# Where the sums of the second weights are made: three quarters moved between VectorE, GpSimd and their places in the order

## The chip, the cores and the metric

The kernel runs on one core of a Trainium2 chip. The metric is the device time of one execution in microseconds (us). The kernel before takes 844.11 us, the median of three runs (843.39, 844.11, 844.64). Five engines work side by side: PE (TensorE, the matmuls), DVE (VectorE), ACT (ScalarE), POOL (GpSimd) and SP (SyncE, which here issues nearly all DMA transfers, one after the other in program order).

## What is computed

Attention inside chunks of 64 positions, then a residual feed-forward layer behind a normalisation, all in float32:

```python
# q, k, v: 8 batches x 8 heads x 576 positions x 64
scores = scale * np.matmul(q_c, k_c.transpose(0, 1, 2, 4, 3))   # 9 chunks of 64
attn = np.exp(scores - np.max(scores, axis=-1, keepdims=True))
attn = attn / (np.sum(attn, axis=-1, keepdims=True) + 1e-09)
x = heads side by side of np.matmul(attn, v_c)                  # 8 x 576 x 512
mu = np.mean(x, axis=-1, keepdims=True)
var = np.mean((x - mu) ** 2, axis=-1, keepdims=True)
xn = (x - mu) / np.sqrt(var + 1e-06) * g_ln
ch = np.maximum(xn @ w_ch1, 0.0) @ w_ch2                        # 512 -> 2048 -> 512
return x + ch
```

(The line on x is put in words.)

## The kernel before

**Tiles.** The 4608 rows are 18 pairs of 256 rows, two pairs to a tile of 512. Every float32 product is made as three products of a high and a low part (high by high, high by low, low by high), so each operand needs a cast to its high part on ACT and a subtraction for its low part on VectorE or GpSimd.

**The plain tiles.** The first three tiles run the feed-forward layer as it stands: for each of 16 blocks of 128 hidden features, `up` makes 12 matmuls into a PSUM bank h (L561), `split` makes its high part hh on ACT (L574) and its low part hl on VectorE (L575), and `down` makes 12 matmuls out of both into the four sums y (L585). There are two banks h, which some of the products of attention (L405) share.

**The units.** The other six tiles run two at a time in three "units" (`unit_ffn`), in which the weights and rows are cut into 2 x 2 blocks and seven block products do the work of eight. The first weights' products stand at L1016 with the rows' operands xc, the second weights' in `double` at L944. This needs sums and differences of weight blocks, made once and kept in DRAM: those of the first weights by `prepare` (tiles `sums` and `parts` on GpSimd, stored to `wa`), those of the second weights by `mix`, to `wb`. The second weights themselves are stored as well (`w2d`).

**A quarter's sums.** The 16 second weights make eight pairs, p = 0 to 7. `mix(p, engine, pool, tag, again)` makes the sums of one pair, called a "quarter" here as in the change's own words, in a 128 x 2048 tile `mixed` that takes the place `tag` of a weight that is no longer needed. In its order: two additions of high and low part (L984, 128x512), four differences and sums of blocks (L991, 128x256), two casts on ACT (L995), two low parts (L998), four stores to `wb` (L1002). The engine named makes the eight that aren't casts. With `again` the blocks are first loaded from `w2d` (L979), as the weights' own places are taken by then. Each `next` of the generator does one step: a load (only with `again`), an addition, an addition, two differences, two more, the casts, a low, a low, the stores.

**Attention of a later pair** runs in between: scores (PE L305 into the bank s), their maximum (`top`, VectorE L312), the subtraction of it (`p_sb`, L337), which frees s, the exponential (ACT L340), 16 transposes on VectorE (L376 into `pt_sb`), the product with v (PE L405, into the banks h or into s), the row sums (`den`, L383 to L385), the division (L431 or L439 into x), mean and variance (L449, L450, `vare` L454), 1/sqrt on GpSimd (`rstd`, L455), the normalised rows (`xg`, VectorE L461; ACT L467), and their transposes on PE through the same bank s (L493). There is one bank s, so the transposes of one block of rows wait until `p_sb` of the other block has been read. `combine` (streams P and Q) then makes the operands xc of the unit from these rows: casts on ACT (L782), low parts on GpSimd (L786), differences on VectorE (L789).

**What sets the order.** All engines run in program order, and the program is laid out by hand. `layout` writes the plain feed-forward of a tile as a list of tokens (u1: an up with its split, u: a down), and the table THIRD gives, by the position of a token in that list, the letters of the streams of which one step goes in front of it. In the last plain tile C, D, G and H are the attention of pairs to come, S is `prepare`, a, b, c, d, T, U and V are quarters of the second weights, P and Q are `combine`. The eighth quarter, and what remains of Q, is woven into the first unit by the table MIX_STEPS (positions in the unit's running count of work). `operand` names the weights' places in which the seven operands xc lie. In the last unit `double.place` puts some of the high and low parts for the second products into the places w3 and w4 as well (L866 to L881).

| stream | quarter | engine and place before | after |
|---|---|---|---|
| a | 1 | VectorE, w0 | VectorE, w0 |
| b | 2 | GpSimd, w1 | GpSimd, w1 |
| c | 3, then 0 | VectorE, w2 | VectorE, w9, loaded again |
| d | 0, then 3 | VectorE, w9, loaded again | GpSimd, w10, loaded again, in the first unit |
| T | 4 | GpSimd, raw | GpSimd, w4 |
| U | 5 | GpSimd, raw | GpSimd, raw |
| V | 6 | GpSimd, w7 | GpSimd, w8 |
| in the unit | 7 | GpSimd, w13 | GpSimd, w13, later in the unit |

Of the kernel before, what the change touches and what calls it, by code (L numbers as in the profile page):

```python
# [10 lines left out]
F32R = mybir.dt.float32r  # L11
# [16 lines left out]
NF = DFF // P  # L28
# [27 lines left out]
AT_END = (0, 6, 11, 18, 33, 37, 40, 48, 54, 82, 92, 97, 104, 109, 121, 133, 146)  # L56
PAIR_STEPS = (STEPS, BY_TENSOR, WIDE, AT_END)
HALVES = ((512, 8), (612, 10))
MIX_STEPS = (24, 26, 30, 34, 54, 60, 62, 76)
REST = (2, 6, 20)  # L60


# [41 lines left out]
def chunk_attention_ffn(ctx: ExitStack, tc: tile.TileContext, qkv, v01, g, w, out):  # L104
    nc = tc.nc
    PSUM = bass.MemoryType.PSUM

    const = ctx.enter_context(tc.tile_pool(name="const", bufs=1))
# [7 lines left out]
    raws = ctx.enter_context(tc.tile_pool(name="raws", bufs=1))  # L116
# [547 lines left out]
    def prepare():  # L664
        late = []
        for p in range(NF // 2):
            fe, q, e = 2 * p, p // 2, p % 2
            both = [wp[fe], wp[fe + 1]]
            t_ = raws.tile([P, 2, 2, PAIR], F32, name="sums", tag="wf")
            for i in range(2):  # L670
                nc.gpsimd.tensor_tensor(
                    out=t_[:, i], in0=both[i][:, 0, :DM].rearrange("p (a n) -> p a n", a=2).bitcast(F32),
                    in1=both[i][:, 1, :DM].rearrange("p (a n) -> p a n", a=2).bitcast(F32), op=ALU.add,
                )
            for i in range(2):
                nc.sync.dma_start(w2d[fe + i], both[i][:, :, DM:].bitcast(F32))
            yield
            a11, a12, a21, a22 = t_[:, 0, 0], t_[:, 0, 1], t_[:, 1, 0], t_[:, 1, 1]
            nc.gpsimd.tensor_tensor(out=a22, in0=a21, in1=a22, op=ALU.add)
            nc.gpsimd.tensor_tensor(out=a21, in0=a11, in1=a21, op=ALU.subtract)  # L680
            nc.gpsimd.tensor_tensor(out=a11, in0=a22, in1=a11, op=ALU.subtract)
            nc.gpsimd.tensor_tensor(out=a12, in0=a12, in1=a11, op=ALU.subtract)
            for to, of in late:
                nc.sync.dma_start(to, of.bitcast(F32))
            nc.sync.dma_start(wa[q][:, e, 0], both[0][:, :, PAIR:DM].bitcast(F32))
            nc.sync.dma_start(wa[q][:, e, 1], both[0][:, :, :PAIR].bitcast(F32))
            nc.sync.dma_start(wa[q][:, 6, e], both[1][:, :, PAIR:DM].bitcast(F32))
            yield
            yield
            r = raws.tile([P, 2, 2, 2, PAIR], F32R, name="parts", tag="raw")  # L690
            nc.scalar.copy(r[:, 0], t_)
            yield
            nc.gpsimd.tensor_tensor(out=r[:, 1], in0=t_, in1=r[:, 0].bitcast(F32), op=ALU.subtract)
            late = [
                (wa[q][:, 2 + e, 0], r[:, :, 0, 0]), (wa[q][:, 4 + e, 1], r[:, :, 0, 1]),
                (wa[q][:, 4 + e, 0], r[:, :, 1, 0]), (wa[q][:, 2 + e, 1], r[:, :, 1, 1]),
            ]
            yield
        for to, of in late:
            nc.sync.dma_start(to, of.bitcast(F32))  # L700
        yield
# [42 lines left out]
    def start_ring():  # L744
        t_ = const.tile([P, 2, 2 * DM], F32R, name="ring", tag="w7")
        ring.add(t_[:, 0], t_[:, 1])
        yield
        for c in "hl":
            t_ = xtp.tile([P, 2, 2 * DM], F32R, name="ring", tag=f"xt{c}")
            ring.add(t_[:, 0], t_[:, 1])  # L750
        yield

    shared = {}
# [5 lines left out]

    def operand(name):  # L760
        if name not in shared:
            shared[name] = const.tile([P, 2, 2, 2 * PAIR], F32R, name="xc", tag=f"w{'2165734'.index(name)}")
        return shared[name]

    def combine(u, half):
# [207 lines left out]
    def mix(p, engine, pool, tag, again=False):  # L973
        both = pool.tile([P, 2, 2, DM], F32, name="mixed", tag=tag)
        t_, his = ([both[:, i, k] for k in range(2)] for i in range(2))
        if again:
            blocks = [[t_[k], his[k]] for k in range(2)]
            for k in range(2):
                nc.sync.dma_start(both[:, :, k], w2d[2 * p + k])  # L979
            yield  # L980
        else:
            blocks = [[x[:, DM:].bitcast(F32) for x in weights(2 * p + k)] for k in range(2)]
        for k in range(2):
            engine.tensor_tensor(out=t_[k], in0=blocks[k][0], in1=blocks[k][1], op=ALU.add)  # L984
            yield
        b11, b12, b21, b22 = (t_[k // 2][:, k % 2 * PAIR : (k % 2 + 1) * PAIR] for k in range(4))
        for k, (out, x, y, op) in enumerate((
            (b11, b12, b11, ALU.subtract), (b12, b22, b12, ALU.subtract), (b22, b11, b22, ALU.subtract),
            (b21, b21, b22, ALU.add),
        )):  # L990
            engine.tensor_tensor(out=out, in0=x, in1=y, op=op)  # L991
            if k % 2:
                yield
        for k in range(2):
            nc.scalar.copy(his[k].bitcast(F32R), t_[k])  # L995
        yield
        for k in range(2):
            engine.tensor_tensor(out=t_[k].bitcast(F32R), in0=t_[k], in1=his[k], op=ALU.subtract)  # L998
            yield
        for k in range(2):  # L1000
            for h, x in enumerate((his, t_)):
                nc.sync.dma_start(wb[:, p, h, 2 * k : 2 * k + 2], x[k].rearrange("p (a n) -> p a n", a=2))  # L1002
        yield
# [139 lines left out]
    tiles = [Tokens(t) for t in range(NTILE)]  # L1143
# [8 lines left out]
    with tc.manual_schedule():  # L1152
        nc.scalar.activation(minus, ident, AF.Copy, scale=-1.0)
        play(START, now)
        now.update(
            A=now.pop("E"), B=tiles[2].attention(1), C=tiles[3].attention(0, True), D=tiles[4].attention(0, True),
            G=tiles[3].attention(1), H=tiles[4].attention(1, True, pt_raw=True), S=prepare(), R=start_ring(), T=mix(4, nc.gpsimd, raws, "raw"),
            U=mix(5, nc.gpsimd, raws, "raw"), V=mix(6, nc.gpsimd, const, "w7"), a=mix(1, nc.vector, const, "w0"),
            b=mix(2, nc.gpsimd, const, "w1"), c=mix(3, nc.vector, const, "w2"), d=mix(0, nc.vector, const, "w9", True),
            X=bring(range(2 * LEAD - 2, 2 * LEAD)), P=combine(0, 0), Q=combine(0, 1),  # L1160
        )
        now.update(zip("u1", tiles[1].ffn(0, 2, room=ROOMS[1])))
        play(layout(ROOMS[1], SECOND), now)
        streams = {}

        def following(u, n):
            n, u = n % 4, u + n // 4
            if (u, n) not in streams and u < UNITS:
                by_pe = len(PAIR_STEPS[n]) == len(BY_TENSOR)
                streams[u, n] = tiles[LEAD + 2 * u + n % 2].attention(n // 2, pt_by_pe=by_pe)  # L1170
            return streams.get((u, n), iter(" "))

        now["N"] = following(1, 0)
        now.update(zip("u1", tiles[2].ffn(0, 2, room=ROOMS[2])))
        play(layout(ROOMS[2], THIRD, True), now)
        side = [(at, now["Q"]) for at in REST]
        stream = mix(NF // 2 - 1, nc.gpsimd, const, "w13")
        side += [(at, stream) for at in MIX_STEPS]
        for u in range(UNITS):
            if u + 1 < UNITS:  # L1180
                for n in range(4):
                    begin, steps = BEGINS[n], PAIR_STEPS[n]
                    side += [(begin + at, following(u + 1, n)) for at in steps]
                    side.append((begin + steps[0], following(u + 1, n + 1)))
                for half, (begin, step) in enumerate(HALVES):
                    stream = combine(u + 1, half)
                    side += [(begin + i * step, stream) for i in range(13)]
            side = weave(unit_ffn(u), side)
        assert not side
# [35 lines left out]
```

## Time and profile before

| | |
|---|---|
| median of three runs | 844.11 us (843.39 to 844.64) |
| the profiled execution | 843.47 us |
| its span, first to last instruction | 841.7 us |
| mean granted TensorE clock | 0.991 |
| PE busy | 821.6 us (98%), 6746 matmuls |
| PE's weight loads | 715.5 us (85%) |
| VectorE busy | 635.9 us (76%), 1007 instructions |
| ScalarE busy | 347.2 us (41%) |
| GpSimd busy | 195.1 us (23%), 164 instructions |

Times in the trace count from the span's start. By stages, each row is a stretch, its length, then busy time and number of instructions of PE, PE's weight loads, VectorE, ACT and GpSimd, the granted clock, the share of the DMA engines and GB/s. These are the stretches of the second plain tile's end, the last plain tile and the rest:

```profile
160.00:220.00 60.00, 60.00 (x503) 49.20 (x502) 45.32 (x83) 15.17 (x22) 31.85 (x29) 1.00 0.70 241
220.00:344.00 124.00, 113.59 (x881) 91.88 (x883) 90.10 (x135) 40.27 (x67) 75.05 (x67) 0.94 0.62 216
344.00:510.00 166.00, 166.00 (x1498) 150.29 (x1488) 142.14 (x229) 77.72 (x131) 33.37 (x20) 1.00 0.79 259
```

A row of the timeline has the start, the length of the group, the engine, the line, the operation, what it writes and reads, how many instructions, and in brackets the idle time before it with the engine, tile and line that ended it. A row of the waits has who waited for whom, the sum, the number of times and the longest. A row of the chain of waits has start, length and what ran, along the one path of work that ended last.

### The profile page before, as it was taken

The numbers are of one execution on the slowest core, as the hardware profiler recorded it, in microseconds if no ns is written. First come the engines' busy times: TensorE is split into PE (matmuls) and PEld (weight loads), VectorE is DVE, ScalarE is ACT, GpSimd is POOL, SyncE is SP. The second block draws the span as 40 slices with busy tenths as digits, with TensorE's granted clock in tenths as the row PEclk, the third lists the DMA queues.
The fourth block names the chain that finished last, engine by engine and source line by source line (L and its number), as shares of the span: only waits on it lengthen the run. The fifth ranks groups of instructions, "written<-read, shape, count | busy, mean of one in ns | idle before, by whom it ended". The sixth has DMA issues, their size and how long they took to land.

```text
span 841.7 us, 17010 instructions
## 1 busy us (share of the span) xinstructions
PE 821.6 (98%) x6746; PEld 715.5 (85%) x6746; DVE 635.9 (76%) x1007; ACT 347.2 (41%) x553; POOL 195.1 (23%) x164
## 2 busy tenths in 40 slices
PE   7999999999997799999999999999999999999998
PEld 5888888888885688888899998788999988889998
DVE  6999966787566896779788998888789952349854
ACT  4776431122323143343455463434555532245432
POOL 0111006473767464510000270000002700000000
PEclk9999999999998899999999999999999999999999
DMA  9997407948983447988878669787787586668662
GB/s 359 333 289 209 167 34 259 308 159 287 329 283 128 139 145 271 322 289 274 289 239 295 223 185 342 244 275 229 248 285 240 177 288 191 195 200 276 208 218 101
DMA packets 119583, 200.63 MB, mean 238 GB/s; under 512 B 9040, under 2 KB 76112, under 8 KB 117584
## 3 DMA queue, kind: packets, MB, share of 16 engines
q1 hardware_dynamic: 118208, 194.82, 68.6%
q0 software_dynamic: 1296, 4.72, 2.9%
q8 instruction: 53, 0.87, 0.4%
q14 instruction: 26, 0.21, 0.1%
HBM read 141.84 MB, written 48.76 MB: 226 GB/s over the span
## 4 chain that ended last, share of the span: by engine, by line
PE 86%; DVE 8%; DMA 2%; POOL 1%; SPq 1%; ACT 1%; issue 0%; DVEq 0%; POOLq 0%; ACTq 0%
PE y L944 29%; PE y L1016 26%; PE y L585 13%; PE h L561 13%; PE s L305 2%; DVE pt_sb L376 2%; PE h L405 1%; DVE mixed L991 1%; DMA wp<-wfs 1%; DMA k_t<-qkv 1%; DVE xg L461 1%; DMA wa<-wp 1%; DVE hl L575 0%; PE s L405 0%; PE s L331 0%
## 5 line engine op out<-in xcount | busy, mean ns | idle before, releaser
L1016 PE MATMUL y<-xc,ring 128*128 128x512 f32 x1008 | 235.1, 392 | 0.2 <-DVE hu L1025 0.2
L1016 PEld LDWEIGHTS y<-xc,ring 128*128 128x128 f32 x1008 | 187.5, 188 | 39.8 <-DVE hu L1025 0.6
L944 PE MATMUL y<-ring,hx 128*128 128x256 f32 x1272 | 158.0, 283 | 0.0
L944 PEld LDWEIGHTS y<-ring,hx 128*128 128x128 f32 x1272 | 155.0, 192 | 0.0
L561 PE MATMUL h<-xth,wp 128*128 128x512 f32 (+1 forms) x432 | 129.6, 370 | 0.3 <-DMA wp<-wfs 0.2
L1025 DVE TENSOR_TENSOR hu<-y,snap 128x512 f32<-128x512 f32 x72 | 49.2, 686 | 69.0 <-PE y L1016 34.7
L585 PE MATMUL y<-wp,hh 128*128 128x512 f32 x376 | 99.3, 404 | 0.0
L881 ACT ACTIVATE hx<-hu 128x512 fp32r<-128x512 f32 x106 | 65.8, 630 | 65.8 <-PE y L944 60.9
L786 POOL TENSOR_TENSOR xc<-rows,xc 128x512 fp32r<-128x512 f32 x28 | 60.1, 2158 | 135.3 <-ACT xc L782 133.7
L561 PEld LDWEIGHTS h<-xth,wp 128*128 128x128 f32 x432 | 78.3, 188 | 14.9 <-DVE hl L575 0.6
L585 PEld LDWEIGHTS y<-wp,hh 128*128 128x128 f32 x376 | 71.3, 194 | 14.6
L890 DVE TENSOR_TENSOR hx<-hu,hx 128x512 fp32r<-128x512 f32 x90 | 67.5, 759 | 14.9 <-ACT hx L881 13.2
L561 PE MATMUL h<-xtl,wp 128*128 128x512 f32 (+1 forms) x216 | 78.3, 367 | 0.0
L575 DVE SCALAR_TENSOR_TENSOR hl<-h,hh 128x512 fp32r<-128x512 f32 (+1 forms) x53 | 32.9, 628 | 58.0 <-ACT hh L574 57.8
L574 ACT ACTIVATE hh<-h 128x512 fp32r<-128x512 f32 (+1 forms) x53 | 28.5, 544 | 114.1 <-PE h L561 114.1
L1022 ACT COPY snap<-y 128x512 f32<-128x512 f32 x72 | 41.7, 585 | 73.4 <-PE y L1016 73.4
L944 PE MATMUL y<-ring,hh 128*128 128x256 f32 x496 | 71.8, 283 | 0.0
L944 PEld LDWEIGHTS y<-ring,hh 128*128 128x128 f32 x496 | 65.2, 192 | 0.2
L585 PE MATMUL y<-wp,hl 128*128 128x512 f32 x188 | 52.2, 392 | 0.0
L881 ACT ACTIVATE hh<-hu 128x512 fp32r<-128x512 f32 x62 | 38.8, 631 | 31.5 <-PE y L944 29.1
L455 POOL TENSOR_TENSOR rstd<-vare,mhalf 128x2 f32<-128x2 f32 x12 | 9.7, 805 | 180.6 <-DVE vare L454 180.6
L376 DVE STREAM_TRANSPOSE pt_sb<-p_sb 32x256 f32<-32x256 f32 x112 | 48.8, 436 | 3.6 <-ACT p_sb L340 1.7
(146 smaller groups left out, 1096.5 us busy)
## 6 DMA issues: line engine op xcount, KB each, us to landing
ring<-wa SPq DMA_DIRECT2D x84, 512.0 KB, 4.5
ring<-wb SPq DMA_DIRECT2D x48, 512.0 KB, 3.7
ring<-w2d SPq DMA_DIRECT2D x36, 512.0 KB, 4.0
raw<-w SPq DMA_DIRECT2D x15, 1024.0 KB, 7.6
out<-x SPq DMA_DIRECT2D x22, 512.0 KB, 5.6
q_t<-qkv SPq DMA_DIRECT2D x17, 512.0 KB, 5.5
k_t<-qkv SPq DMA_DIRECT2D x17, 512.0 KB, 6.8
v_t<-qkv SPq DMA_DIRECT2D x32, 256.0 KB, 6.8
```

The source lines that it names most:

```text
L376: nc.vector.transpose(out=pt_sb[quad(2 * h2 + j), :, c, quad(i)], in_=p_sb[quad(2 * c + i), :, h2, quad(j)])
L561: nc.tensor.matmul(h, lhsT=(wh, wh, wl)[m][:, ks], rhs=(xth, xtl, xth)[m][:, k, :], start=i == 0, stop=i == len(terms) - 1,)
L574: nc.scalar.activation(hh, h, AF.Relu)
L575: nc.vector.scalar_tensor_tensor(out=hl, in0=h, scalar=0.0, in1=hh.bitcast(F32), op0=ALU.max, op1=ALU.subtract)
L585: nc.tensor.matmul(sums(pairs[j // 2])[j % 2], lhsT=(hh, hh, hl)[m], rhs=(wh, wl, wh)[m], start=f == 0 and m == 0, stop=f == NF - 1 and m ...
L786: engine.tensor_tensor(out=o[:, 1], in0=x, in1=o[:, 0].bitcast(F32), op=ALU.subtract)
L881: nc.scalar.activation(hh, self.split[i][2], AF.Relu if x == "1" else AF.Copy)
L890: nc.vector.tensor_tensor(out=hl, in0=x, in1=hh.bitcast(F32), op=ALU.subtract)
L944: nc.tensor.matmul(bank[j // 2][:, j % 2 * PAIR : (j % 2 + 1) * PAIR], lhsT=(hh, hh, hl)[m][:, j * P : (j + 1) * P], rhs=loaded[t // 2][:, ...
L1016: nc.tensor.matmul(bank, lhsT=w[:, (0, 0, 1)[m], ks], rhs=x[:, (0, 1, 0)[m], k, :], start=start and k == m == 0, stop=k == 1 and m == 2, s ...
L1022: nc.scalar.copy(out, bank)
L1025: nc.vector.tensor_tensor(out=out, in0=bank, in1=s, op=ALU.add)
```

## The change

It leaves PE's order as it is and changes where the sums of the second weights stand.

- Stream a (VectorE, quarter 1): its five steps up to the casts stand together at position 3, where they were spread over positions 4 to 8, and its lows and stores at 6.
- VectorE's second quarter in this tile was c, quarter 3, at positions 9 to 16. Now c is quarter 0, which was d: it loads its blocks again at 20 and runs at 24 to 28.
- Quarter 3 goes to GpSimd: it is loaded at position 23 and made in the first unit, from 8 on, ahead of quarter 7, which begins at 64.
- GpSimd's quarters T, U, V and b stand some positions later or earlier, T in w4 in place of `raw`, V in w8 in place of w7.
- The seven operands xc lie in other places of the same weights.

```diff
 THIRD = {
-    0: "CS", 1: "CS", 2: "DDGS", 3: "DS", 4: "aaDDS", 5: "aaDS", 6: "aDGSbb", 7: "aaGGHSbbTT", 8: "aDGTT", 9: "ccDb",
+    0: "CS", 1: "CS", 2: "DDGS", 3: "DSaaaaa", 4: "DDS", 5: "DS", 6: "aaaDGS", 7: "GGHSbb", 8: "DGbb", 9: "Db",
...
-MIX_STEPS = (24, 26, 30, 34, 54, 60, 62, 76)
+MIXING = (8, 64)
+MIX_STEPS = (0, 2, 6, 10, 32, 40, 42, 56)
...
-    tag=f"w{'2165734'.index(name)}"
+    tag=f"w{'3621457'.index(name)}"
...
-    T=mix(4, nc.gpsimd, raws, "raw"), V=mix(6, nc.gpsimd, const, "w7"),
-    c=mix(3, nc.vector, const, "w2"), d=mix(0, nc.vector, const, "w9", True),
+    T=mix(4, nc.gpsimd, const, "w4"), V=mix(6, nc.gpsimd, const, "w8"),
+    c=mix(0, nc.vector, const, "w9", True), d=mix(3, nc.gpsimd, const, "w10", True),
...
-        stream = mix(NF // 2 - 1, nc.gpsimd, const, "w13")
-        side += [(at, stream) for at in MIX_STEPS]
+        for stream, begin in zip((now["d"], mix(NF // 2 - 1, nc.gpsimd, const, "w13")), MIXING):
+            side += [(begin + at, stream) for at in MIX_STEPS]
```

In the changed kernel every line number past 58 is higher by one.

VectorE's order where the first quarter stands, in the first blocks of the last plain tile, before (`mixed` is the quarter, `hl` the low part of a hidden block, `x` to `xg` the attention of one block of rows, `top` and `p_sb` that of the next):

```order
L385 RECIPROCAL rden<-den 128x16
L575 SCALAR_TENSOR_TENSOR hl<-h,hh 128x512
L984 TENSOR_TENSOR mixed<-wp 128x512 x2
L431 TENSOR_TENSOR x<-s,rden 128x2x8x64
...
L454 TENSOR_SCALAR vare<-mv 128x2
L991 TENSOR_TENSOR mixed<-mixed 128x256 x4
L461 SCALAR_TENSOR_TENSOR xg<-x,mv,g_sb 128x512 x2
L575 SCALAR_TENSOR_TENSOR hl<-h,hh 128x512
L998 TENSOR_TENSOR mixed<-mixed 128x512 x2
L312 TENSOR_REDUCE top<-s 128x16
L337 TENSOR_TENSOR p_sb<-s,top 128x2x8x64
```

The same place after:

```order
L386 RECIPROCAL rden<-den 128x16
L985 TENSOR_TENSOR mixed<-wp 128x512 x2
L992 TENSOR_TENSOR mixed<-mixed 128x256 x4
L576 SCALAR_TENSOR_TENSOR hl<-h,hh 128x512
L432 TENSOR_TENSOR x<-s,rden 128x2x8x64
...
L455 TENSOR_SCALAR vare<-mv 128x2
L462 SCALAR_TENSOR_TENSOR xg<-x,mv,g_sb 128x512 x2
L576 SCALAR_TENSOR_TENSOR hl<-h,hh 128x512
L999 TENSOR_TENSOR mixed<-mixed 128x512 x2
L313 TENSOR_REDUCE top<-s 128x16
L338 TENSOR_TENSOR p_sb<-s,top 128x2x8x64
```

The six first sums now stand ahead of the hl that was ahead of them; the two lows kept their place.

VectorE's order a block later, where the second quarter (c) began, before:

```order
L575 SCALAR_TENSOR_TENSOR hl<-h,hh 128x512
L984 TENSOR_TENSOR mixed<-wp 128x512 x2
L575 SCALAR_TENSOR_TENSOR hl<-h,hh 128x512
L991 TENSOR_TENSOR mixed<-mixed 128x256 x4
L376 STREAM_TRANSPOSE pt_sb<-p_sb 32x8x32 x16
L575 SCALAR_TENSOR_TENSOR hl<-h,hh 128x512
L383 TENSOR_REDUCE den<-p_sb 128x16
```

And after:

```order
L576 SCALAR_TENSOR_TENSOR hl<-h,hh 128x512 x2
L377 STREAM_TRANSPOSE pt_sb<-p_sb 32x8x32 x16
L576 SCALAR_TENSOR_TENSOR hl<-h,hh 128x512
L384 TENSOR_REDUCE den<-p_sb 128x16
L385 TENSOR_SCALAR den<-den 128x16
```

The six sums are gone from here, and the 16 transposes stand directly behind two hl.

GpSimd's order at the end of the last plain tile and in the first unit, before (`xc` are the low parts of the unit's operands):

```order
L786 TENSOR_TENSOR xc<-rows,xc 128x2x256 x5
L595 TENSOR_TENSOR rstd<-vare,mhalf 128x2 x2
L786 TENSOR_TENSOR xc<-rows,xc 128x2x256 x3
L984 TENSOR_TENSOR mixed<-wp 128x512 x2
L991 TENSOR_TENSOR mixed<-mixed 128x256 x4
L998 TENSOR_TENSOR mixed<-mixed 128x512 x2
L455 TENSOR_TENSOR rstd<-vare,mhalf 128x2 x4
```

And after:

```order
L596 TENSOR_TENSOR rstd<-vare,mhalf 128x2 x2
L787 TENSOR_TENSOR xc<-rows,xc 128x2x256 x2
L985 TENSOR_TENSOR mixed<-mixed 128x512 x2
L992 TENSOR_TENSOR mixed<-mixed 128x256 x4
L787 TENSOR_TENSOR xc<-rows,xc 128x2x256
L999 TENSOR_TENSOR mixed<-mixed 128x512 x2
L985 TENSOR_TENSOR mixed<-wp 128x512 x2
L992 TENSOR_TENSOR mixed<-mixed 128x256 x4
L456 TENSOR_TENSOR rstd<-vare,mhalf 128x2
L999 TENSOR_TENSOR mixed<-mixed 128x512 x2
L456 TENSOR_TENSOR rstd<-vare,mhalf 128x2 x3
```

One quarter before stands between the last xc and the first rstd; after, a second one stands ahead of it, its first six sums ahead of the last xc.

More of the change, by code (lines that the diff above doesn't have):

```diff
@@ L44 @@
 THIRD = {
-    0: "CS", 1: "CS", 2: "DDGS", 3: "DS", 4: "aaDDS", 5: "aaDS", 6: "aDGSbb", 7: "aaGGHSbbTT", 8: "aDGTT", 9: "ccDb",
-    10: "ccGGPbbbT", 11: "HGGTT", 12: "cGTUU", 13: "GPUU", 14: "GGHP", 15: "ccGHPU", 16: "cGHPUU", 17: "GPUVV",
-    18: "HHGPVV", 19: "HGP", 20: "HGPV", 21: "HHPVVd", 22: "HPV", 24: "H", 25: "ddH", 26: "ddQQ", 27: "QR", 28: "dQ",
-    29: "ddQXXN", 30: "dQQR", 31: "Q",
+    0: "CS", 1: "CS", 2: "DDGS", 3: "DSaaaaa", 4: "DDS", 5: "DS", 6: "aaaDGS", 7: "GGHSbb", 8: "DGbb", 9: "Db",
+    10: "bbTTGGP", 11: "TTHGGPb", 12: "G", 13: "GT", 14: "TTGGHPUU", 15: "GHPTUU", 16: "GHP", 17: "UGP",
+    18: "UUHHGPVV", 19: "UHGPVV", 20: "HGPc", 21: "HHPV", 22: "HPVV", 23: "Vd", 24: "ccH", 25: "ccH", 26: "cQQ",
+    27: "ccQR", 28: "cQ", 29: "QXXN", 30: "QQR", 31: "Q",
 }
@@ L761, in operand @@
         if name not in shared:
-            shared[name] = const.tile([P, 2, 2, 2 * PAIR], F32R, name="xc", tag=f"w{'2165734'.index(name)}")
+            shared[name] = const.tile([P, 2, 2, 2 * PAIR], F32R, name="xc", tag=f"w{'3621457'.index(name)}")
         return shared[name]
@@ L1156, in chunk_attention_ffn @@
             A=now.pop("E"), B=tiles[2].attention(1), C=tiles[3].attention(0, True), D=tiles[4].attention(0, True),
-            G=tiles[3].attention(1), H=tiles[4].attention(1, True, pt_raw=True), S=prepare(), R=start_ring(), T=mix(4, nc.gpsimd, raws, "raw"),
-            U=mix(5, nc.gpsimd, raws, "raw"), V=mix(6, nc.gpsimd, const, "w7"), a=mix(1, nc.vector, const, "w0"),
-            b=mix(2, nc.gpsimd, const, "w1"), c=mix(3, nc.vector, const, "w2"), d=mix(0, nc.vector, const, "w9", True),
+            G=tiles[3].attention(1), H=tiles[4].attention(1, True, pt_raw=True), S=prepare(), R=start_ring(), T=mix(4, nc.gpsimd, const, "w4"),
+            U=mix(5, nc.gpsimd, raws, "raw"), V=mix(6, nc.gpsimd, const, "w8"), a=mix(1, nc.vector, const, "w0"),
+            b=mix(2, nc.gpsimd, const, "w1"), c=mix(0, nc.vector, const, "w9", True), d=mix(3, nc.gpsimd, const, "w10", True),
             X=bring(range(2 * LEAD - 2, 2 * LEAD)), P=combine(0, 0), Q=combine(0, 1),
```

## The prediction

> **What bounds the kernel now.** I began with TensorE's waits over the whole run, since the page has PE busy for 98% of the span. Besides the start there are two large ones, both in the last plain tile (220 to 344 us), and both on VectorE:
>
> ```profile
> PE s L493 <- DVE p_sb L337: 5.5, 1, 5.5
> PE h L405 <- DVE hl L575: 4.0, 1, 4.0
> ```
>
> PE's own timeline shows where they stand, and that the matmuls behind them are slow too:
>
> ```profile
> 236.24 1.07 PE L585 MATMUL y<-wp,hl 128*128 128x512 f32 x4
> ...
> 253.16 0.39 PE L561 MATMUL h<-xth,wp 128*128 128x512 f32 x1
> 259.04 1.09 PE L493 MATMUL s<-ident,xg 128*128 128x128 f32 x4 [5.50 <-DVE p_sb L337]
> ...
> 276.42 1.07 PE L585 MATMUL y<-wp,hl 128*128 128x512 f32 x4
> 277.78 0.33 PE L405 MATMUL h<-v_t,pt_sb 64*64 64x64 f32 x2 [0.29 <-DVE pt_sb L376]
> 278.70 0.33 PE L405 MATMUL h<-v_t,pt_sb 64*64 64x64 f32 x2 [0.59 <-DVE pt_sb L376]
> 283.04 1.97 PE L405 MATMUL h<-v_t,pt_sb 64*64 64x64 f32 x60 [4.02 <-DVE hl L575]
> ```
>
> The chain of waits has the same kinds of work behind a gap and away from one (the last three rows are the fast ones), and two of VectorE's sums, alone and beside GpSimd:
>
> ```profile
> 247.34 0.43 DVE mixed L991
> ...
> 248.26 2.50 DVE mixed L991
> ...
> 260.13 4.67 PE y L585 x12
> 264.80 0.44 PE s L493 x4
> ...
> 285.01 4.37 PE y L585 x12
> ...
> 294.85 2.72 PE y L585 x12
> ...
> 303.90 1.09 PE s L405 x64
> ```
>
> So the first gap costs 5.50 idle, 1.09 - 0.44 and 4.67 - 2.72: **8.1 us**. The second costs 0.29 + 0.59 + 4.02 idle, 0.33 + 0.33 + 1.97 - 1.09 for its 64 matmuls, and 4.37 - 2.72 behind them: **8.1 us**. Everything later runs on PE almost without a wait.
>
> Why VectorE is late there, its timeline says:
>
> ```profile
> 242.01 0.69 DVE L575 SCALAR_TENSOR_TENSOR hl<-h,hh 128x512 fp32r<-128x512 f32 x1 [5.07 <-ACT hh L574]
> 242.62 1.28 DVE L984 TENSOR_TENSOR mixed<-wp 128x512 f32<-128x512 f32 x2
> 243.82 1.22 DVE L431 TENSOR_TENSOR x<-s,rden 128x1024 f32<-128x1024 f32 x1
> ...
> 246.89 3.87 DVE L991 TENSOR_TENSOR mixed<-mixed 128x256 f32<-128x256 f32 x4
> 250.69 3.49 DVE L461 SCALAR_TENSOR_TENSOR xg<-x,mv,g_sb 128x512 f32<-128x512 f32 x2
> ...
> 254.69 1.80 DVE L998 TENSOR_TENSOR mixed<-mixed 128x512 fp32r<-128x512 f32 x2
> 256.42 1.21 DVE L312 TENSOR_REDUCE top<-s 128x16 f32<-128x1024 f32 x1
> 257.67 1.22 DVE L337 TENSOR_TENSOR p_sb<-s,top 128x1024 f32<-128x1024 f32 x1
> ...
> 268.73 0.69 DVE L575 SCALAR_TENSOR_TENSOR hl<-h,hh 128x512 fp32r<-128x512 f32 x1 [6.71 <-ACT hh L574]
> 269.34 5.80 DVE L991 TENSOR_TENSOR mixed<-mixed 128x256 f32<-128x256 f32 x4
> 275.06 7.21 DVE L376 STREAM_TRANSPOSE pt_sb<-p_sb 32x256 f32<-32x256 f32 x16
> ...
> 294.66 1.41 DVE L461 SCALAR_TENSOR_TENSOR xg<-x,mv,g_sb 128x512 f32<-128x512 f32 x2
> ```
>
> Ahead of p_sb, which PE waits for, stand all eight sums of the first quarter; ahead of the transposes stand four of the second. Just before each stretch VectorE was idle, 5.07 and 6.71 us, waiting for an hh that depends on PE. GpSimd makes both stretches longer: L991 took 0.43 alone and 2.50 while `parts` ran, the xg pair 3.49 instead of 1.41.
>
> ```profile
> 247.06 0.81 POOL L455 TENSOR_TENSOR rstd<-vare,mhalf 128x2 f32<-128x2 f32 x1 [8.01 <-DVE vare L454]
> 247.84 2.64 POOL L693 TENSOR_TENSOR parts<-sums,parts 128x1024 fp32r<-128x1024 f32 x1
> ...
> 350.30 1.29 POOL L786 TENSOR_TENSOR xc<-rows,xc 128x512 fp32r<-128x512 f32 x1 [8.76 <-ACT xc L782]
> 351.55 2.54 POOL L984 TENSOR_TENSOR mixed<-wp 128x512 f32<-128x512 f32 x2
> 354.04 3.21 POOL L991 TENSOR_TENSOR mixed<-mixed 128x256 f32<-128x256 f32 x4
> 357.21 2.55 POOL L998 TENSOR_TENSOR mixed<-mixed 128x512 fp32r<-128x512 f32 x2
> ```
>
> **The change part by part** (times on the clock of before).
>
> *First quarter into the idle 5.07 us.* Its first sum still waits until PE has finished with weight 0, whose place it takes: 236.24 + 1.07 = 237.3. Two sums (1.28) and four (4 x 0.43 = 1.72) end at 240.3, a microsecond later if GpSimd's last sums for the first weights are in their way. What is queued behind is the hl of 242.01, so the new wait delays little: two ACT casts that now stand ahead of its hh can cost up to 0.9. x then starts at 242.6 to 243.5 instead of 243.82. From x to the end of vare it is 3.1 (243.82 to 246.89): 245.7 to 246.6. The four L991 are gone from here. xg follows at once: 1.41 alone, 3.49 beside GpSimd. rstd and `parts` follow vare on GpSimd, 0.81 + 2.64, until 249.3 to 250.2. hl (0.69) is ready by then. The two lows L998 stay; the first must wait out `parts` as the L991 of 2.50 did, so I let them end 1.7 after it, at 251.0 to 251.9. With top 1.21 and p_sb 1.22: 253.4 to 254.3. PE arrives at 253.16 + 0.39 = 253.55. Left over of the gap: 0 to 0.9, and 2 if xg is held as well. I take 0.5, near the uncontended row, since GpSimd sat idle 8.01 us before rstd and can't be ahead of xg. **-8.1 + 0.5.**
>
> This also puts the four stores of the quarter ahead of the v, q and k loads in SP's queue: those are now issued once the lows have ended, at 251 to 252. PE's scores out of that q and k ran at 270.65, and will at 262.5 without the first gap:
>
> ```profile
> 270.65 1.16 PE L305 MATMUL s<-k_t,q_t 64*64 64x64 f32 x64
> ```
>
> That leaves 10 us for the loads, so I cost it at nothing.
>
> *Second quarter off VectorE here.* After the hl of 268.73 (0.6) the transposes start at 269.3, not 275.06, and end 7.2 later at 276.6; the hl behind them (0.69) at 277.3. PE reaches these products at 276.42 + 1.07 = 277.5. Both ends hang on the same matmuls of PE, so this holds wherever the first gap ends. Left over: 0 to 0.5, taken as 0.2. **-8.1 + 0.2.** The third of VectorE's quarters, made from the stored weights, becomes its second one, on VectorE still and about two blocks from the tile's end, a few instructions earlier among the hl; no wait stood there, and I cost it at 0.
>
> *Quarters 2, 4, 5 and 6 on GpSimd* keep their instructions. The places w4 and w8 in place of `raw` and w7 remove a wait for stores; the xc operands that are needed first lie in places without a quarter. Both are off PE's path: 0.
>
> *A quarter more on GpSimd in the first unit.* 2.54 + 3.21 + 2.55 = 8.3 us. Its first six sums fit into the 8.76 us in which GpSimd waited for a cast at 350.30, so the last xc low isn't late. Its load from DRAM stands in SP's queue before the unit. What it can cost is through VectorE, which is held by it and busy here for 69 of 86 us:
>
> ```profile
> 344.00:430.00 86.00, 86.00 (x833) 70.37 (x823) 69.10 (x119) 34.47 (x58) 11.74 (x12) 1.00 0.83 276
> ```
>
> Between 0 (VectorE's idle 16.9 us cover it) and 8.3; by the quarter that stands here now without a PE wait I take 0.3.
>
> *Places w3 and w4 in the last unit.* ACT's first cast into w4 must now wait for PE's last first-half product:
>
> ```profile
> 753.27 1.16 ACT L881 ACTIVATE hx<-hu 128x512 fp32r<-128x512 f32 x2 [0.33 <-PE y L1016]
> ...
> 757.23 17.87 PE y L944 x149
> ```
>
> It moves from 753.27 to 757.2, and its low on VectorE to some 758.6. PE wants them for the third pair of products, 2 x 24 x 0.12 = 5.8 after 757.23. Covered by about 4 us: 0, at worst 1.
>
> Sum against the profiled execution of 843.47: 843.47 - 8.1 + 0.5 - 8.1 + 0.2 + 0.3 = 828.3. The median of the three runs lies 0.64 above that execution, and I expect the same of the new kernel: **828.9**.
>
> [...] The L991 at 247.34 took 0.43 while GpSimd's rstd (247.06 to 247.87) was at work. [...]
>
> After a shorter wait, near the start, 64 matmuls took 1.16 us, close to the 1.09 of the fast row:
>
> ```profile
> 14.72 1.16 PE L305 MATMUL s<-qk_b 64*64 64x64 f32 x64 [1.11 <-ACT p_sb L335]
> ```
>
> After 5.50 idle the loss to the clock is 2.6 us (0.65 and 1.95). [...]
>
> **Rivals.**
>
> *A, part of the first gap stays.* GpSimd takes its turns ahead of xg and both lows. Against it: GpSimd follows vare. For it: 3.49 and 2.50. p_sb would be 2 to 4 us after PE: 830.5 to 833.
>
> *B, the second gap stays.* ACT's two casts of GpSimd's quarter 2 now stand before the hh of that hl. GpSimd ends those sums near 256 (250 + 2.5 + 3.2), PE wants the hh about 260. From 4 us late on, each microsecond is lost; the whole gap back is 837.
>
> *C, slower.* In the first unit GpSimd holds VectorE through two quarters instead of one, and PE waits for VectorE's additions out of PSUM. All of 2 x 8.3 = 16.6 us on PE, with the clock lost as in the first gap (8.1 / 5.5), is 24.5: 843.5 - 16.2 + 24.5 = 851.8, or 852.4 as a median. It decides from 16.2 x 5.5 / 8.1 = 11 us of these 16.6 on. Against it: one quarter stands there now and PE waits for VectorE's additions 0.2 us in all (the last column):
>
> ```profile
> L1016 PE MATMUL y<-xc,ring 128*128 128x512 f32 x1008 | 235.1, 392 | 0.2 <-DVE hu L1025 0.2
> ```
>
> *D, given back at the tile's end.* The stores of the last VectorE quarter stand before the loads of x, q and k in SP's queue; if its lows come late, PE waits at the unit's start, up to all of the gain: about 844. Against it: its lows come a few instructions earlier than before, and the list of waits, which goes down to 0.2 us, has none of PE there.
>
> That the sums don't move is excluded: the order shows them moved.
>
> **How the numbers follow.** Forecast 0.66, A 0.17, B 0.10, C 0.03, D 0.04. Range: the lower end is both gaps gone without leftover or later cost, 843.47 - 16.2 = 827.3, less 0.5 for the spread of runs (843.39 to 844.64): 826.8. The upper end holds A and the nearer half of B: 834.5. What lies outside is C, D and about half of B. Within 0.2% (842.4 to 845.8, what a measurement of this kernel can't tell from no change) falls half of D: 0.02; slower is C, 0.03; the rest, 0.95, is faster.
>
> **What would show it.** Right: no wait of PE on p_sb or hl above 1 us between 230 and 300, the granted clock at full there, VectorE's six first sums before the hl at 242, transposes directly behind an hl, the unit's start near 326. Wrong: a p_sb wait of 2 us or more (A), ACT casts of `mixed` ending after the up that its hh belongs to (B), PE waits on L1025 in the first unit (C), or on x or k loads at its start (D).

## The result

The changed kernel takes 831.79 us (median of four runs, 831.56 to 833.12); the kernel before, run beside it, takes 843.75. The ratio is 0.986, with a 95% interval of 0.9843 to 0.9877: 12.0 us or 1.4% faster. The profiled execution took 831.56, its span is 829.8 (841.7 before), and its mean granted clock 1.000 (0.991 before).

**Waits.** TensorE's waits of the changed kernel (who waited for whom, sum, times, longest). Every line number is one higher than before:

```profile
PE h L406 <- DMA v_t<-qkv: 1.9, 1, 1.9
PE s L494 <- DVE p_sb L338: 1.2, 1, 1.2
...
PE s L365 <- ACT p_sb L341: 0.4, 1, 0.4
```

The wait on hl (4.0) and those on pt_sb (0.9) are gone, the wait on p_sb has shrunk from 5.5 to 1.2. The first and the third row are new, and both stand in the first unit. TensorE's timeline:

```profile
253.37 0.39 PE L562 MATMUL h<-xth,wp 128*128 128x512 f32 x1
254.95 0.63 PE L494 MATMUL s<-ident,xg 128*128 128x128 f32 x4 [1.20 <-DVE p_sb L338]
255.34 2.10 PE L586 MATMUL y<-wp,hh 128*128 128x512 f32 x8
...
270.98 1.16 PE L406 MATMUL h<-v_t,pt_sb 64*64 64x64 f32 x64
...
360.14 1.09 PE L365 MATMUL s<-ident,p_sb 128*128 128x128 f32 x8 [0.37 <-ACT p_sb L341]
...
407.43 0.69 PE L406 MATMUL h<-v_t,pt_sb 64*64 64x64 f32 x32 [1.88 <-DMA v_t<-qkv]
408.36 0.69 PE L406 MATMUL h<-v_t,pt_sb 64*64 64x64 f32 x32 [0.23 <-issue]
```

Behind the 1.20 us the granted clock stays at 1.00 (behind the 5.50 of before it was 0.50), and the second place (270.98) has no wait at all.

**VectorE** at the two places:

```profile
237.55 1.83 DVE L985 TENSOR_TENSOR mixed<-wp 128x512 f32<-128x512 f32 x2 [0.38 <-PE y L586]
239.30 2.34 DVE L992 TENSOR_TENSOR mixed<-mixed 128x256 f32<-128x256 f32 x4
242.83 0.69 DVE L576 SCALAR_TENSOR_TENSOR hl<-h,hh 128x512 fp32r<-128x512 f32 x1 [1.18 <-ACT hh L575]
...
246.50 1.41 DVE L462 SCALAR_TENSOR_TENSOR xg<-x,mv,g_sb 128x512 f32<-128x512 f32 x2
...
248.43 3.98 DVE L999 TENSOR_TENSOR mixed<-mixed 128x512 fp32r<-128x512 f32 x2
252.34 1.21 DVE L313 TENSOR_REDUCE top<-s 128x16 f32<-128x1024 f32 x1
253.58 1.23 DVE L338 TENSOR_TENSOR p_sb<-s,top 128x1024 f32<-128x1024 f32 x1
...
262.91 7.21 DVE L377 STREAM_TRANSPOSE pt_sb<-p_sb 32x256 f32<-32x256 f32 x16
```

The six first sums now lie in what was idle time ahead of the hl (which moved by 0.8, from 242.01 to 242.83). xg takes 1.41. What still holds p_sb up is the pair of lows: 3.98 us, where the same pair took 1.80 in the kernel before (254.69, beside GpSimd's L991) and the shortest low of this trace 0.68. GpSimd was at work on its own sums all the while:

```profile
246.68 1.13 POOL L456 TENSOR_TENSOR rstd<-vare,mhalf 128x2 f32<-128x2 f32 x1 [6.69 <-DVE vare L455]
247.78 2.39 POOL L694 TENSOR_TENSOR parts<-sums,parts 128x1024 fp32r<-128x1024 f32 x1
250.13 3.43 POOL L985 TENSOR_TENSOR mixed<-wp 128x512 f32<-128x512 f32 x2
```

One by one, the first low took 2.29 and ended at 250.72, half a microsecond behind `parts`. The second took 1.77, beside the first of the two L985 (250.13 to 251.87).

**Where the time went.** TensorE's order is the same in both kernels, so the start of the same scores (L305, L306) in the two traces shows what was gained up to there; these starts are the landmarks of all that follows. Three of these rows of the changed kernel:

```profile
264.22 1.16 PE L306 MATMUL s<-k_t,q_t 64*64 64x64 f32 x64
...
369.35 1.16 PE L306 MATMUL s<-k_t,q_t 64*64 64x64 f32 x64
...
392.38 1.16 PE L306 MATMUL s<-k_t,q_t 64*64 64x64 f32 x64
```

| scores at (before) | at (after) | gained so far | what lies between |
|---|---|---|---|
| 246.72 | 246.93 | -0.21 | start of the run |
| 270.65 | 264.22 | 6.43 | first gap: +6.64 |
| 343.39 | 328.55 | 14.84 | second gap: +8.41 |
| 383.56 | 369.35 | 14.21 | first unit, the wait on p_sb: -0.63 |
| 512.55 | 500.79 | 11.76 | first unit, the wait for v_t and the matmuls behind it: -2.46 |
| end of span 841.7 | 829.8 | 11.9 | nothing more |

So 15.05 us were won in the last plain tile, and 3.09 lost again in the first unit. The prediction had 15.5 and 0.3.

**The load behind the wait for v_t.** In the kernel before, SP issued the load that belongs to this place at 409.13, and TensorE took up the product without a wait:

```profile
409.13 1.67 SPq L322 DMA_DIRECT2D v_t<-qkv  x2
```

```profile
419.69 1.16 PE L405 MATMUL h<-v_t,pt_sb 64*64 64x64 f32 x64
```

But its first half had landed only at 419.15, so this load had about half a microsecond in hand. It was issued 2.5 us after the scores that ran at 406.60. In the changed kernel it was issued at 398.19, 5.8 us after the same scores (392.38), and its first half landed at 407.29, 1.7 us after TensorE was ready for it (407.43 less the 1.88 of wait).

### The profile page after: what moved, and what is told of

The parts are those of the page before. It is cut to its first block, busy times and chain, and to the rows that moved or that the text cites. A ratio compares the mean times of both kernels' runs of the same rounds, so it can differ in the third digit from the quotient of the medians.

```text
span 829.8 us, 17018 instructions
## 1 busy us (share of the span) xinstructions
PE 816.0 (98%) x6746; PEld 711.7 (86%) x6746; DVE 627.4 (76%) x999; ACT 346.6 (42%) x553; POOL 204.1 (25%) x172
## 4 chain that ended last, share of the span: by engine, by line
PE 86%; DVE 8%; DMA 4%; issue 1%; ACT 1%; SPq 1%; POOL 0%; DVEq 0%; ACTq 0%
PE y L945 29%; PE y L1017 22%; PE y L586 15%; PE h L562 14%; PE s L306 2%; DMA v_t<-qkv 2%; DVE pt_sb L377 2%; PE h L406 1%; DMA wp<-wfs 1%; DMA k_t<-qkv 1%; DVE hu L1026 1%; PE s L406 1%; DVE stats L450 1%; DVE top L313 1%; DVE mixed L999 0%
## 5 line engine op out<-in xcount | busy, mean ns | idle before, releaser
L586 PE MATMUL y<-wp,hh 128*128 128x512 f32 x376 | 96.2, 394 | 0.0
L586 PEld LDWEIGHTS y<-wp,hh 128*128 128x128 f32 x376 | 69.1, 188 | 13.9
```

What stands on the lines that cost most here:

```text
L586: nc.tensor.matmul(sums(pairs[j // 2])[j % 2], lhsT=(hh, hh, hl)[m], rhs=(wh, wl, wh)[m], start=f == 0 and m == 0, stop=f == NF - 1 and m ...
```

## The experiments

All of them are read by the same landmarks. Each column is a difference of the "gained so far" between two scores; the start of the run is taken off, as it differs from one execution to the next by over 4 us (the scores of 246.93 start at 245.93 in the change's second execution and at 250.17 with the first quarter back, where TensorE waits 1.3 us for the first k and 2.6 for weights). Each row is one profiled execution. The first three columns repeat to within 0.1 wherever the program is the same there; the fourth does not, as the last row shows, so single differences of a microsecond in it are not secured.

| run | first gap | second gap | unit, p_sb | unit, later | sum |
|---|---|---|---|---|---|
| the change | +6.64 | +8.41 | -0.63 | -2.46 | 11.96 |
| first quarter alone | +6.69 | +1.61 | 0 | -0.75 | 7.55 |
| first quarter back | +0.70 | +8.41 | -0.60 | -1.60 | 6.91 |
| lows behind p_sb | +8.02 | +8.42 | -0.61 | -2.42 | 13.41 |
| GpSimd's queue | +6.65 | +8.41 | -0.46 | -0.99 | 13.61 |
| two stores | +6.64 | +8.42 | -0.63 | -2.21 | 12.22 |
| v loads earlier | +6.69 | +8.41 | -0.60 | -1.63 | 12.87 |
| without quarter 3 | +6.69 | +8.41 | -0.06 | -1.55 | 13.49 |
| lows and v | +8.02 | +8.42 | -0.62 | -1.05 | 14.77 |
| casts earlier | +6.69 | +8.41 | 0 | -2.40 | 12.70 |
| lows and casts | +8.02 | +8.41 | 0 | -0.40 | 16.03 |
| all three | +8.03 | +8.41 | 0 | -1.15 | 15.29 |
| the change again | +6.69 | +8.42 | -0.62 | -3.86 | 10.63 |

### The two parts, each alone

The kernel before with only the first quarter moved up (of a line of the table THIRD, the diffs show the entries that differ):

```diff
-    3: "DS", 4: "aaDDS", 5: "aaDS", 6: "aDGSbb", 7: "aaGGHSbbTT", 8: "aDGTT",
+    3: "DSaaaaa", 4: "DDS", 5: "DS", 6: "aaaDGSbb", 7: "GGHSbbTT", 8: "DGTT",
```

> Only the first quarter is moved up; the second stays on VectorE ahead of the transposes. If the two gaps are separate (my theory), PE's wait on p_sb shrinks from 5.5 to about 1.2 us and the wait on hl stays at 4.0: 843.75 - 6.6 = 837.1 us. If both come from one backlog on VectorE, so that ending the first delay also shortens the second (rival), the hl wait falls under 2 us and the time to 833 or less.

It took 835.48 us (before beside it 844.98; ratio 0.9885, 0.9861 to 0.9909). The first gap closed as expected, but the second did not stay as it was. VectorE and TensorE there:

```profile
263.70 1.79 DVE L991 TENSOR_TENSOR mixed<-mixed 128x256 f32<-128x256 f32 x4
265.40 7.21 DVE L376 STREAM_TRANSPOSE pt_sb<-p_sb 32x256 f32<-32x256 f32 x16
```

```profile
273.39 1.15 PE L405 MATMUL h<-v_t,pt_sb 64*64 64x64 f32 x60 [1.29 <-DVE hl L575]
...
287.01 1.94 PE L585 MATMUL y<-wp,hl 128*128 128x512 f32 x4 [2.26 <-DVE hl L575]
```

The four sums ahead of the transposes are still there, but they take 1.79 us where they took 5.80: with the first gap gone they fall into a stretch in which GpSimd is idle (257.85 to 265.43; in the kernel before it was at work from 269.28 to 276.29, beside all four). The wait on hl falls to 1.29. A new one of 2.26 comes later, behind it the granted clock falls to 0.50, and the sum over the tile is 8.3 (6.69 + 1.61). The rival is half right: the wait at the second place hung mostly on the first gap, but the time came back later.

The new wait has another source than VectorE's quarter. The hl that ends it stands behind a difference of `combine`, which waited for GpSimd's xc, and GpSimd had waited for stores to leave the place `raw`:

```profile
281.35 2.54 POOL L984 TENSOR_TENSOR mixed<-wp 128x512 f32<-128x512 f32 x2 [4.02 <-DMA wb<-mixed]
```

```profile
285.16 1.20 DVE L789 TENSOR_TENSOR rows<-rows 128x512 f32<-128x512 f32 x1 [5.57 <-POOL xc L786]
```

The change gives quarter 4 the place w4, and its trace has no wait of GpSimd for stores here (its waits between 257 and 283 are 3.34 us for an ACT cast, 1.81 for TensorE and 1.22 for VectorE). So with the first gap closed, part of the second column's 8.41 belongs to GpSimd's new places and order and not to VectorE's quarter; no run takes these apart.

The changed kernel with the first quarter back:

```diff
-    3: "DSaaaaa", 4: "DDS", 5: "DS", 6: "aaaDGS", 7: "GGHSbb", 8: "DGbb",
+    3: "DS", 4: "aaDDS", 5: "aaDS", 6: "aDGS", 7: "aaGGHSbb", 8: "aDGbb",
```

> The changed kernel with the first quarter back at its old positions. My theory: the p_sb wait of about 5.5 us is back, the second gap stays away, the later loss (PE waits 1.9 us for v_t in the first unit) stays too: 831.8 + 6.6 = 838.4 us. Rival (GpSimd's other order, not the early first quarter, cured part of the first gap): under 836.

838.17 us (ratio 0.9916, 0.9889 to 0.9943), with the 5.5 us on p_sb back. As expected; GpSimd's other order is worth 0.70 at the first gap. In the tile the two parts alone are worth 8.3 and 9.1, both together 15.05: 2.4 us are counted in both.

### What is left of the first gap

```diff
-    6: "aaaDGS", 7: "GGHSbb",
+    6: "DGS", 7: "GGaaaHSbb",
```

> The changed kernel with the first quarter's two low parts behind top and p_sb on VectorE (their stores then stand behind the v loads). If the remaining 1.2 us of the first gap are the 3.98 us that these two lows took beside GpSimd, the p_sb wait is gone: 830.5 us, from 831.8. If GpSimd holds top and p_sb in their place (rival), the wait stays near 1 us and the time near 831.8.

831.02 us (0.9833, 0.9813 to 0.9853). The wait on p_sb in the tile is gone and the gap is worth 8.02; the interval overlaps that of the change, so for the whole run the gain is not secured:

```profile
249.97 1.23 DVE L338 TENSOR_TENSOR p_sb<-s,top 128x1024 f32<-128x1024 f32 x1
251.11 2.86 DVE L999 TENSOR_TENSOR mixed<-mixed 128x512 fp32r<-128x512 f32 x2
```

p_sb now ends at 251.2, some 2.7 us ahead of TensorE, and the lows are slow (2.86) where nobody waits for them. The gap in the kernel before was thus 8.0 us, as the prediction had it (8.1).

### What is lost in the first unit

The stores of the two quarters made there, on GpSimd's queue:

```diff
-                nc.sync.dma_start(wb[:, p, h, 2 * k : 2 * k + 2], x[k].rearrange("p (a n) -> p a n", a=2))
+                (queue or nc.sync).dma_start(wb[:, p, h, 2 * k : 2 * k + 2], x[k].rearrange("p (a n) -> p a n", a=2))
```

(Quarters 3 and 7 are made with `queue=nc.gpsimd`, the others as they were.)

> The changed kernel with the stores of the two quarters that are made in the first unit issued by GpSimd instead of SP, the same bytes. If PE's wait for v_t (1.9 us near 407) is the four more stores ahead of that load in SP's queue (my theory), the wait is gone and the time is 831.8 - 2.4 = 829.4 us. If it is the bandwidth or the landing of the transfers (rival), the wait stays and the time is 831.8 or more.

832.03 us (0.9856, 0.9824 to 0.9889). By the landmarks the loss falls from 2.46 to 0.99, but a wait of 0.8 us for v_t stays, and the runs show no gain. SP has eight issues less ahead of the v load and still gets to it no earlier (399.44, after 398.19); what shrank is the time from its issue to its landing (7.2 us, after 9.1). So my theory did not hold as it stood. The next three runs ask how much is issue and how much transfer. Each quarter stored in two pieces in place of four:

```diff
-        for k in range(2):
-            for h, x in enumerate((his, t_)):
-                nc.sync.dma_start(wb[:, p, h, 2 * k : 2 * k + 2], x[k].rearrange("p (a n) -> p a n", a=2))
+        for h in range(2):
+            nc.sync.dma_start(wb[:, p, h], both[:, 1 - h].rearrange("p k (a n) -> p (k a) n", a=2))
```

> The changed kernel with the four stores of each quarter made as two of twice the size, the same bytes. If the v_t load comes late because SP spends about 0.55 us on each issue ahead of it (theory I), a quarter's stores take some 1.2 us of SP instead of 2.3 and the PE wait for v_t falls from 1.9 to about 0.8 us: 830.7. If the full DMA engines make it late (theory B, after the run with the stores on GpSimd's queue still had 0.8 us of that wait), the wait stays at 1.5 us or more: 831.5 to 832.

832.0 us (0.9854, 0.9839 to 0.987). SP's queue in the changed kernel, and then in this one (start, time that the issues took):

```profile
361.31 2.24 SPq L1003 DMA_DIRECT2D wb<-mixed  x4
363.59 3.36 SPq L481 DMA_DIRECT2D rows<-x  x4
367.06 0.52 SPq L721 DMA_DIRECT2D ring<-wa  x1
367.64 2.50 SPq L481 DMA_DIRECT2D rows<-x  x4
...
398.19 1.10 SPq L323 DMA_DIRECT2D v_t<-qkv  x2
```

```profile
361.55 0.85 SPq L1002 DMA_DIRECT2D wb<-mixed  x2
362.45 4.05 SPq L481 DMA_DIRECT2D rows<-x  x4
366.60 1.13 SPq L721 DMA_DIRECT2D ring<-wa  x1
367.77 2.51 SPq L481 DMA_DIRECT2D rows<-x  x4
...
398.42 1.18 SPq L323 DMA_DIRECT2D v_t<-qkv  x2
```

The stores took 1.4 us less of SP (0.85 against 2.24), the issues behind them 1.3 us more (4.05 and 1.13 against 3.36 and 0.52), and the v load was issued at the same time. So what SP spends on a quarter's stores does not set when the v load is issued, and theory I fell. Single issues got longer instead (one load of the ring, the weights for the unit, took 1.13 where it had taken 0.52), with the DMA engines busy for 0.88 of the time from 364 to 368 in the change's trace. That it is the transfers that hold SP here is the likely reading; no run shows it directly.

The v loads ahead of the next pair's q and k:

```diff
+        if moved:
+            v_t = [load.tile([P, HP, 2, D], F32, name="v_t", bufs=2) for _ in range(2)]
+            for j in range(2):
+                nc.sync.dma_start(v_t[j], qkv[pair, :, 2, j * DM : (j + 1) * DM])
         s2 = banks()
...
-        else:
+        elif not moved:
             v_t = [load.tile([P, HP, 2, D], F32, name="v_t", bufs=2) for _ in range(2)]
```

> The changed kernel with the v loads of the pairs from 10 on issued in the step of the scores, ahead of the next pair's q and k loads (1 MB) instead of behind them. By both theories v_t lands 3 to 5 us earlier and PE's wait for it in the first unit is gone: 831.8 - 2.4 = 829.4 us. If v_t has to wait for its place (the v product of the pair before) it stays at 831.8.

830.44 us (0.984, 0.9824 to 0.9855). The wait for v_t is gone, and TensorE waits 1.4 us for a weight of the ring in its place, as that was loaded behind v_t; of the 2.46 only 0.83 is won back.

Without quarter 3 (`d` is never stepped, so its sums are left out; quarter 2 is stored twice):

```diff
-                nc.sync.dma_start(wb[:, p, h, 2 * k : 2 * k + 2], x[k].rearrange("p (a n) -> p a n", a=2))
+                for to in (p, 3) if p == 2 else (p,):
+                    nc.sync.dma_start(wb[:, to, h, 2 * k : 2 * k + 2], x[k].rearrange("p (a n) -> p a n", a=2))
```

> The changed kernel without quarter 3: it is neither loaded nor made, and quarter 2's stores are issued a second time in its place in the last plain tile, so this leaves out part of the sums. If the moved quarter is what makes the first unit lose 3.1 us (waits for v_t and for p_sb), both waits are gone: 828.7. If the shorter plain tile alone makes them (rival: less time for the same transfers; the run with the first quarter alone had 0.45 us of wait for v_t and no moved quarter), half or more of the 2.5 us of loss at v_t stays: 830 or more.

830.93 us (0.9849, 0.9829 to 0.9869). The wait on p_sb is gone, 1.55 of the 2.46 at v_t stay, as the rival had it. By this one execution the moved quarter itself accounts for some 0.6 and 0.9. The run of the first quarter alone, whose unit is that of the kernel before, lost 0.75 here behind a tile that was 8.3 us shorter, and the run with the first quarter back 1.60 where the change lost 2.46, behind a tile 6 us longer. All three point the same way, that a shorter tile alone makes the load late; each is one execution.

### The casts, and what adds up

The lows behind p_sb together with the earlier v loads:

> The changed kernel with both corrections: the first quarter's lows behind p_sb and the v loads ahead of the next q and k. If the two leftovers are separate, their gains add: 831.8 - 1.4 - 2.4 = 828.0 us. If the time won in the tile is lost again in the first unit (rival: the transfers set the pace there), 829.4 or more.

829.68 us (0.9825, 0.9808 to 0.9841), nearer to the rival. The tile keeps its gain, the unit loses 1.67 (0.62 and 1.05, now mostly a wait of 0.8 on a `snap`, the copy of a product that ACT makes for VectorE's next addition). The profiled execution, 827.89, is the fastest of its four.

What makes the wait on p_sb in the unit, ACT's timeline of the changed kernel says:

```profile
351.98 1.33 ACT L468 ACTIVATE xg<-xg,rstd 128x512 f32<-128x512 f32 x2 [2.40 <-POOL rstd L456]
353.22 1.12 ACT L996 CAST mixed<-mixed 128x512 fp32r<-128x512 f32 x2
354.25 0.58 ACT L1023 COPY snap<-y 128x512 f32<-128x512 f32 x1
```

Quarter 7's two casts, which the new MIX_STEPS put here, stand between xg and the snap that VectorE's next addition needs; top, p_sb and the exponential stand behind that. ACT had been idle for 2.40 us just before. The casts moved into that idle time:

```diff
-            side += [(begin + at, stream) for at in MIX_STEPS]
+            side += [(begin + (20 if begin > 8 and at == 32 else at), stream) for at in MIX_STEPS]
```

> The changed kernel with the two ACT casts of quarter 7 moved up by 12 steps in the first unit, ahead of ACT's xg instead of behind it. Their 1.12 us stand there ahead of a snap for which VectorE waits, with top, p_sb and the rows transfers behind. If these casts are a part of the loss in the first unit (theory C), the PE wait on p_sb (0.4 us) is gone, SP reaches the rows transfers 1.1 us earlier, and the wait for v_t falls from 1.9 to about 0.8 us: 830.1 us. If it is the bytes alone (theory B), only the p_sb part goes: 831.2 or more.

830.85 us (0.9845, 0.9825 to 0.9865). The wait on p_sb is gone, as both theories had it, but the later stretch still loses 2.40: the wait for v_t is 1.60, where theory C had 0.8, and 0.54 are lost ahead of it, before the scores at 392.60. With only the lows moved, 1.14 of the 2.42 were lost in that same stretch ahead of the load (0.68 of it a wait on a snap at 383.91).

> The changed kernel with the first quarter's lows behind p_sb and the casts of quarter 7 ahead of xg. By theory C 831.8 - 1.4 - 1.7 = 828.7 us; by theory B 829.8 or more, since what is won in the tile is lost at v_t.

829.81 us (0.9834, 0.9814 to 0.9855). The median is what theory B had. But by the landmarks of the profiled execution (828.07, the fastest of its five) both gaps are closed and the unit loses only 0.40. Its program for the unit is word for word that of the run before it.

> All three corrections: lows behind p_sb, v loads ahead of the next q and k, casts ahead of xg. If the wait on snap or on a ring load (0.8 to 1.4 us, which took the place of the wait for v_t) also hangs on the casts, all of the 3.1 us lost in the first unit is won back: 831.8 - 1.4 - 3.0 = 827.4 us, faster than both kernels. If it is the transfers' pace: 828.5 to 829.5.

829.08 us (0.9826, 0.9806 to 0.9845), inside the range of the transfers' pace, with 1.15 lost in the unit, 0.9 of it a wait for the ring.

The three combinations have medians of 829.1 to 829.8 where the change has 831.8. Only the first of them (0.9808 to 0.9841) lies, and just so, wholly below the change's interval (0.9843 to 0.9877), so that a faster version than both kernels is likely but not secured.

The change once more:

> The changed kernel once more, unchanged. Two kernels whose program for the first unit is the same, word for word, lost 2.4 and 0.4 us there (with the casts moved, without and with the lows moved). If the order of the program sets that loss, this execution loses the same 3.1 us in the first unit as the one before (0.6 at p_sb, 2.5 at v_t). If the landing of the transfers through full DMA engines sets it, the loss at v_t differs by 0.5 us or more while the 0.6 at p_sb, which hangs on the ACT casts, stays.

831.92 us (0.9858, 0.9835 to 0.9882). The wait on p_sb cost 0.62 again. The wait for v_t repeated as well, 1.90 after 1.88, but the stretch lost 3.86 in place of 2.46, since this time the granted clock fell behind the wait (last section). So neither half of the expectation holds as worded: in these two executions both waits belong to the program, and what differs, by 1.40, is not the landing but the clock.

## Why the prediction was right, and where not

- **First gap into the idle 5.07 us.** Right in the mechanism, 0.7 to 1.0 off in size: 6.64 gained, 7.6 predicted. x started at 243.44, inside the 242.6 to 243.5. The step that was mis-sized is that the lows end 1.7 us after `parts`. It let the first low wait out `parts` and took the second as free. GpSimd went straight on to the next quarter (250.13 above), the second low took 1.77 beside it, the pair ended 2.2 us after `parts`, and 1.20 us were left over, not 0.5. That lies between the prediction's own signs, 1 us for right and 2 us for rival A. The lows behind p_sb show what the pair cost: 8.02. That what is left over costs no more than its own length was my estimate, with one wait of 1.11 us in the trace of before to show for it; it held here, with the clock at 1.00 behind the 1.20.
- **VectorE beside GpSimd.** xg took its 1.41 with rstd at work (246.50 and 246.68), as far as GpSimd's spans, which are rough in this profile, can tell; the L991 of 0.43 beside rstd, in the trace of before, had pointed that way. The lows lost time: 3.98 for the pair, each ending some 0.5 us behind one of GpSimd's instructions (250.72 after 250.17, 252.41 after 251.87).
- **Second quarter off VectorE.** Right: 8.41 where 7.9 was predicted, no wait left. But the two terms of 8.1 were taken as separate, and the run with the first quarter alone shows that they are not. The four sums took 5.80 us because the first gap had put them beside GpSimd; in that run they took their own 1.79, and 1.29 us of wait were left there. A new wait of 2.26 came by way of the place `raw`, and the prediction had put leaving that place at 0. The sum came out right because all of these parts were changed together.
- **The first unit.** This term failed: 0.3 predicted, 3.09 measured, and it makes up most of the difference between 828.9 and 831.79. The step looked at GpSimd's 8.3 us of work and at VectorE beside it. It did not follow ACT and the transfers, which a quarter uses too. ACT's casts came to stand ahead of a snap (0.6, undone by moving them). And the stores of quarter 3, and the later place of quarter 7's stores, came ahead of a load that had half a microsecond in hand even before, and that is late once the tile ahead of it is shorter (2.46; without the quarter 1.55; 0.75 with the unit of the kernel before behind a tile 8.3 us shorter). How the 2.46 divide between the two is argued from single executions. Rival D had the right kind of loss, a load that lands late, but put it at the unit's start and behind VectorE's last quarter.
- **The range.** It is in part luck that 831.79 lies inside: the room up to 834.5 was made for gaps that stay (A and B), and most of what used it up is a loss in the first unit, for reasons that no rival named.
- **The places w3 and w4 in the last unit, and quarters 2, 4, 5, 6.** Cost nothing in the changed kernel, as predicted: from 512.55 on the gain stays as it is to the end.

**Open:** why the same program of the unit lost 2.40 us in the profiled execution with the casts moved and 0.40 in the one with the lows moved as well. Counted from the scores at 369.02 and 367.92, SP reached the v load 2.1 us later in the first (399.01 and 395.79), and the runs don't tell what held it. The first is the slowest of its four executions and the second the fastest of its five. The medians differ by 1.04, no more than the 1.33 that the lows win in the tile, so the 2.0 in the unit may be chance of the two executions.

## What to carry to other kernels

Two gaps that follow each other need not be worth the sum of what each cure wins alone (8.3 and 9.1 here, 15.05 together): close the first and look again. When work is moved off a busy engine, follow every engine and queue that it uses to its new place, its casts, loads and stores too, and ask which transfers the shorter path ahead will now hurry, and which of them land with hardly any time in hand already. Where an engine runs in order, the place of a short step (here two casts of 1.1 us behind xg, or in the idle time ahead of it) can matter more than its length.

## What was not expected of the hardware

The prediction had seen a wait of 1.11 us that cost nothing more and one of 5.50 that did; in these runs the granted clock fell behind one of 1.90. The change's second execution, in stretches of 1 us behind it (the third number from the end is the granted clock):

```profile
407.00:408.00 1.00, 0.93 (x40) 0.81 (x34) 0.13 (x1) 0.00 (x0) 0.00 (x0) 1.00 0.75 225
408.00:409.00 1.00, 1.00 (x4) 0.76 (x4) 1.00 (x2) 0.00 (x0) 0.00 (x0) 0.56 0.84 314
409.00:410.00 1.00, 1.00 (x4) 0.81 (x3) 0.16 (x1) 0.00 (x0) 0.00 (x0) 0.50 0.21 59
410.00:411.00 1.00, 1.00 (x3) 0.78 (x3) 0.00 (x0) 0.55 (x2) 0.00 (x0) 0.50 0.23 49
411.00:412.00 1.00, 1.00 (x5) 0.74 (x4) 0.00 (x0) 1.00 (x3) 0.00 (x0) 0.73 0.98 260
```

The first execution waited 1.88 and then 0.23 at the same place and kept its clock:

```profile
409.00:410.00 1.00, 1.00 (x7) 0.84 (x5) 0.93 (x2) 0.00 (x0) 0.00 (x0) 1.00 0.82 309
410.00:411.00 1.00, 1.00 (x6) 0.79 (x5) 0.36 (x1) 0.31 (x1) 0.00 (x0) 1.00 0.22 62
```

What is missing to a clock of 1.00 in the four slow rows of the second execution adds up to 1.7 us. Waits of 1.20 and 1.29 cost nothing more (0.63 us for the four matmuls behind the one, 1.15 for the 60 behind the other), the one of 2.26 did again (1.94 us for four matmuls that take 1.07). The length of a wait alone does not decide it here, as near its start the same second execution waited 1.94 and its 64 matmuls took the usual 1.16. The mean clock of that whole execution, 0.998 over 830.1 us, leaves some 1.7 us to be missing, and the four slow rows use them up:

```profile
9.17 1.16 PE L306 MATMUL s<-k_t,q_t 64*64 64x64 f32 x64 [1.94 <-DMA k_t<-qkv]
```

So the clock fell behind waits of 1.90 and 2.26 and stayed behind 1.88 and 1.94. What else decides it, no run shows.
